# A planned kernel (attention and two MLPs): later landings in the planner's DMA model, and new tables of priorities and engine choices

## The chip, the cores and the metric

The kernel runs on one core of one Trainium2 chip. The metric is device time in microseconds (us), the median of several runs. Before the change it is 858.77 us (three runs, 855.53 to 861.29).

## The reference, cut to what matters

All data are fp32. There are 4 batches, 8 heads, 576 positions, head width 64 and 32 memory slots.

```
a    = softmax(phi over the 576 positions)              # per batch, head and memory slot
k_m  = a^T k ;  v_m = a^T v                             # 32 x 64 each
attn = softmax(q k_m^T / 8 over the 32 slots) v_m       # 576 x 64 per head
x    = attn as [2304 tokens, 512]
x    = (h * sigmoid(1.702 h)) @ w_out,  h = x @ w_in    # 512 -> 2048 -> 512
xn   = x / rms(x) * rms_g
out  = (silu(xn @ w_gate) * (xn @ w_val)) @ w_o2        # 512 -> 1536 -> 512
```

## The kernel before, in words

The tokens are worked in two pairs of batches (pair 0 and pair 1, 1152 tokens each). The time line has these stages:

- **Attention and first MLP of pair 0** (up to about 240 us). For each batch and half of the heads (a unit, such as (0,1) or (3,0)) the steps `att_k1` to `att_q4` make memory keys and values and then `attnT`. For each of eight groups of 256 hidden columns, `vm_part` folds the memory values into `w_in`, `a_g1` makes the hidden activations, `a_g2` adds into `x2`. Each fp32 operand is split into a high and a low part (the high part a rounded copy on ACT, the low part a subtraction on DVE or POOL), and each product is three matmuls, high by high, low by high and high by low.
- **First MLP of pair 1** (about 240 to 420 us), with the weights read back from `cache_a`. Beside it run pair 0's norm and `t_a`, `t_b`, `t_c`, `t_d`, which form sums and differences of quarters of `x2` and split them into the tiles `tba`, `tbb`, `tbc`, `tbd`.
- **Second MLP of pair 0** (about 420 to 640 us), then of pair 1 (to the end): `s_g3` makes the gated hidden activations of 128 columns by a scheme with seven block products, and `s_g4` multiplies them by `w_o2` and adds into `oacc`; after the last group, `put` writes the output.
- **Weights.** `w_load` (line 731) starts a DMA into one of three `raw` buffers (a strict pool: taken in a fixed order), and `w_conv` (line 766) cleans up the bits: an absolute value on ACT, two TENSOR_SCALARs and two SCALAR_TENSOR_TENSORs, then the split. The second MLP's weights are cleaned during the first MLP (`c`), kept in `cache_b`, combined in `b` and kept in `cache_s`.

**What sets the order.** All steps are first recorded as operations. A planner (class `Plan`) then makes an order for all engines together, and the instructions are issued in that order, engine by engine, each engine in order; what an instruction needs is ensured by semaphores. `cost` (line 361) gives each operation a duration by a formula. `dues` (line 452) gives each a due time: a PE step of the main line is due when its PE turn comes, a side step 20 us (`LAG`) after; then a pass backward makes each operation due early enough for everything that follows from it, or waits for its buffer. `HASTE` takes a number of us off the due time of a step's operations (negative: due later) ahead of that pass. `order` (line 493) walks along the time and, on each engine, takes of the operations that can start the one that is due first. `OTHER` lists, for a step, which of its operations (by number) go to the other one of DVE and POOL.

For a DMA the model is: the transfer starts 1.3 us after its issue, moves at 350 GB/s (224 for 96-partition tiles) one after another, and tells of its landing 0.6 us after the last byte; at most eight are under way.

```
bus = max(bus, t + 1.3) + n / (224e3 if x.ap[0][1] == 96 else 350e3)
u.done = bus + 0.6
```

For a load of 512 KB on an idle bus that is 3.4 us. `fill` (line 576) adds matmuls of `ones_r`, whose result nobody reads, wherever the plan has PE idle before a step that takes a fresh PSUM tile; so these show in the trace where the plan expected PE to stand.

Of the kernel before, what the change touches and what calls it, by code (L numbers as in the profile page):

```python
# [116 lines left out]
class Plan:  # L117
# [5 lines left out]
    SEM = 0.06  # L123
    LAG = 20.0
    FILL = True
    UNIT = {"cache_a": 131072, "cache_b": 65536, "cache_s": 131072}

    HASTE = {
        "a_g1 0 0 1": 8.9,
        "a_g1 0 1 1": 11.5,  # L130
        "a_g1 0 3 0": 26.7,
        "a_g1 0 4 0": 21.9,
        "a_g1 0 4 2": 15.4,
        "a_g1 0 5 0": 20.6,
        "a_g2 0 0 3": 10.5,
        "a_g2 0 1 0": 9.5,
        "a_g2 0 1 1": 13.3,
        "a_g2 0 2 2": 24.1,
        "a_g2 1 5 1": 110.4,
        "att_k1t 1 1": 68.1,  # L140
        "att_k2 2 1": 41.5,
        "att_k3 0 0": 99.0,
        "att_k5 0 1": 38.0,
        "att_k5 2 1": -47.3,
        "att_q3 1 0 0": 45.5,
        "att_q3 1 0 1": 79.0,
        "att_q3s 2 1 0": 3.1,
        "att_q3s 2 1 1": 35.7,
        "att_q3s 3 0 0": 35.3,
        "att_q3s 3 0 1": 54.3,  # L150
        "att_q4 1 0 0": 30.7,
        "att_q4 1 1 0": 43.8,
        "att_q4 2 0 0": 17.4,
        "att_q4 2 1 0": -93.1,
        "norm_1 1 0": 48.0,
        "norm_4 0 0 3": 80.3,
        "norm_4 0 2 3": 123.5,
        "rg": -72.1,
        "s_g3 0 0 1": 19.6,
        "s_g3 1 4 1": 131.2,  # L160
        "s_g4 0 0 1": 26.1,
        "s_g4 0 0 6": 52.3,
        "s_g4 1 1 5": 145.9,
        "s_g4 1 5 7": -42.9,
        "t_b 0 0": 25.2,
        "t_c 0 0": 4.1,
        "vm_part 0 5 0": 29.8,
        "w_conv a 0 0 in 1": 62.1,
        "w_conv a 0 3 out 1": 37.3,
        "w_conv a 0 4 in 0": 32.2,  # L170
        "w_conv b 10 o2": 118.9,
        "w_load a 0 1 out 1": 44.7,
        "w_load a 0 5 in 1": 60.7,
        "w_load b 1 vg": 116.0,
        "w_load c 2 val 1": 115.6,
        "w_load c 3 val 0": 100.1,
    }

    OTHER = {
        "a_g1 0 0 0": (17,),  # L180
        "a_g1 0 0 1": (17,),
        "a_g1 0 1 0": (8,),
        "a_g1 0 1 1": (8,),
        "a_g1 0 1 3": (17,),
        "a_g1 0 2 0": (8, 17),
        "a_g1 0 2 1": (8, 10, 21),
        "a_g1 0 2 2": (8, 10, 19),
        "a_g1 0 3 0": (8,),
        "a_g1 0 3 1": (10,),
        "a_g1 0 3 2": (8, 10, 21),  # L190
        "a_g1 0 3 3": (8, 17),
        "a_g1 0 4 0": (17,),
        "a_g1 0 4 1": (10, 19),
        "a_g1 0 5 0": (17,),
        "a_g1 0 5 1": (10, 19),
        "a_g1 0 5 2": (8, 19, 21),
        "a_g1 0 6 0": (8,),
        "a_g1 0 6 1": (10,),
        "a_g1 0 6 2": (8, 19, 21),
        "a_g1 0 7 1": (8,),  # L200
        "a_g1 1 1 0": (8,),
        "a_g1 1 1 3": (8, 17),
        "a_g1 1 2 1": (21,),
        "a_g1 1 2 3": (17,),
        "a_g1 1 4 1": (21,),
        "a_g1 1 4 2": (8,),
        "a_g1 1 4 3": (17,),
        "a_g1 1 5 0": (8,),
        "a_g1 1 5 1": (19, 21),
        "a_g1 1 5 2": (19, 21),  # L210
        "a_g1 1 6 0": (17,),
        "a_g1 1 6 1": (8, 21),
        "a_g1 1 6 2": (19,),
        "att_k3 1 0": (2,),
        "att_k3 1 1": (2,),
        "att_k3 2 0": (2,),
        "att_k3 2 1": (2,),
        "att_k3s 1 0": (1, 2),
        "att_k3s 1 1": (2,),
        "att_k4 1 0": (27,),  # L220
        "att_k4 1 1": (27,),
        "att_k4 3 0": (27,),
        "att_k4 3 1": (27,),
        "att_q3s 0 0 0": (1,),
        "att_q3s 0 1 0": (1,),
        "att_q3s 0 1 1": (1,),
        "att_q3s 1 0 1": (1,),
        "att_q3s 1 1 1": (1,),
        "att_q3s 2 0 0": (3,),
        "att_q3s 2 0 1": (3,),  # L230
        "att_q3s 2 1 0": (3,),
        "att_q3s 2 1 1": (1, 3),
        "att_q3s 3 0 0": (1, 3),
        "norm_1 0 0": (2,),
        "norm_1 0 1": (5,),
        "norm_1 0 2": (2, 5),
        "norm_1 1 0": (5,),
        "norm_1 1 1": (2, 5),
        "norm_1 1 2": (3, 5),
        "s_g3 0 0 2": (33, 35, 38, 43),  # L240
        "s_g3 0 1 2": (28, 30, 35, 36, 41),
        "s_g3 0 11 2": (31, 33, 35),
        "s_g3 0 2 2": (33, 35, 38, 40, 43),
        "s_g3 0 3 2": (30, 31, 36, 40),
        "s_g3 0 5 2": (40,),
        "t_a 0 0": (1, 3),
        "t_b 0 0": (1,),
        "t_b 0 1": (1,),
        "t_c 0 0": (5,),
        "t_c 0 1": (1, 4, 5, 7),  # L250
        "t_c 1 0": (1, 4),
        "t_c 1 1": (5,),
        "w_conv a 0 0 in 0": (1,),
        "w_conv a 0 0 out 0": (1,),
        "w_conv a 0 0 out 1": (6,),
        "w_conv a 0 1 in 0": (1,),
        "w_conv a 0 1 out 0": (1,),
        "w_conv a 0 1 out 1": (1,),
        "w_conv a 0 2 in 0": (6,),
        "w_conv a 0 2 in 1": (1, 6),  # L260
        "w_conv a 0 2 out 0": (6,),
        "w_conv a 0 3 in 0": (6,),
        "w_conv a 0 3 in 1": (6,),
        "w_conv a 0 3 out 1": (1,),
        "w_conv a 0 4 out 0": (1, 6),
        "w_conv a 0 4 out 1": (1,),
        "w_conv a 0 5 in 1": (1,),
        "w_conv a 0 5 out 0": (1,),
        "w_conv a 0 5 out 1": (1,),
        "w_conv a 0 6 in 1": (1,),  # L270
        "w_conv a 0 6 out 0": (1,),
        "w_conv a 0 6 out 1": (1, 6),
        "w_conv a 0 7 in 1": (6,),
        "w_conv a 0 7 out 0": (1,),
        "w_conv a 0 7 out 1": (1, 6),
# [4 lines left out]
        "w_conv b 3 vg": (2, 3, 11),  # L280
        "w_conv b 4 vg": (2, 5),
        "w_conv b 5 vg": (5,),
        "w_conv b 8 vg": (5,),
        "w_conv c 0 o2 0": (1,),
        "w_conv c 0 val 0": (1,),
        "w_conv c 1 o2 0": (1,),
        "w_conv c 1 o2 1": (1,),
        "w_conv c 1 val 1": (1,),
        "w_conv c 2 gate 0": (1,),
        "w_conv c 2 gate 1": (1,),  # L290
        "w_conv c 2 val 0": (1,),
        "w_conv c 3 gate 0": (1,),
        "w_conv c 3 gate 1": (1,),
        "w_conv c 3 val 0": (1,),
        "w_conv c 3 val 1": (1,),
# [26 lines left out]
    def add(self, op):  # L322
# [6 lines left out]
        for x, write in [(x, False) for x in op.ins] + [(op.out, True)]:  # L329
# [163 lines left out]
    def order(self, until=1e9):  # L493
# [9 lines left out]
        while got < len(units):  # L503
            best = None
            for e in self.ENGINES:
# [20 lines left out]
            t, u = best  # L526
# [18 lines left out]
            if e == "SP":  # L545
                x = u.ops[0].out if u.ops[0].out.space != bass.MemoryType.DRAM else u.ops[0].ins[0]
                n = reduce(int.__mul__, (c for s, c in x.ap), 4)
                bus = max(bus, t + 1.3) + n / (224e3 if x.ap[0][1] == 96 else 350e3)
                u.done = bus + 0.6
                lanes = lanes[1:] + [u.done]  # L550
            for h in u.takes:
                tag = h.tag
# [1234 lines left out]
```

## Time and profile before

| | |
|---|---|
| median of 3 runs | 858.77 us (855.53, 858.77, 861.29) |
| profiled execution | 859.84 us, span 858.1 us, mean granted TensorE clock 0.989 |
| PE busy | 835.6 us (97% of the span), 5785 matmuls |
| DVE busy | 646.2 us (75%) |
| ACT busy | 498.6 us (58%) |
| POOL busy | 288.6 us (34%) |
| DMA | 167.00 MB, mean 195 GB/s |

The span is the time from the first to the last instruction; the execution's own time is 1.7 us longer. An engine is busy while it works on an instruction. For PE, 97% is a union of overlapping matmuls and also counts the matmuls on `ones_r`. The clock is 1.0 at 2.4 GHz and 0.5 at 1.2 GHz.

### The profile page before, as it was taken

To read this page: it belongs to the slowest core of one execution; us is meant where nothing else is said; L and a number is where in the kernel's file an instruction comes from. 1 tells how busy PE (TensorE), PEld (TensorE's weight loads), DVE (VectorE), ACT (ScalarE), POOL (GpSimd) and SP (SyncE) were. 2 spreads that over 40 slices of the span, in tenths; PEclk is the share of its full clock that TensorE was granted. 3 is DMA by queue.
4 is the path that set the end of the run, shared out by engine and by line. 5 is a ranking of instruction groups with operands and counts; after the bars stand their busy time and mean duration, and the time that the engine had idled before them with its cause. 6 is when DMAs were issued, how large, how long until landed. Compare 5 with 4: busy or idle time off the path is not lost.

```text
span 858.1 us, 16008 instructions
## 1 busy us (share of the span) xinstructions
PE 835.6 (97%) x5785; PEld 791.8 (92%) x5785; DVE 646.2 (75%) x1367; ACT 498.6 (58%) x1223; POOL 288.6 (34%) x291
## 2 busy tenths in 40 slices
PE   9999999989999999999899999999999999999997
PEld 7899999989899999999899899999999999999996
DVE  6789999889896898899877698686877434555455
ACT  4698767867688667656577765444444443423321
POOL 4364346786455575746645520000020000000000
PEclk9899999999999999999999999999999999999999
DMA  9965747864975865664775658453544624434403
GB/s 337 270 218 146 251 168 203 265 210 148 303 235 175 263 210 200 238 207 145 253 250 171 234 182 326 150 215 137 216 149 143 216 95 155 170 129 130 159 1 111
DMA packets 76768, 167.00 MB, mean 195 GB/s; under 512 B 7312, under 2 KB 29328, under 8 KB 76688
## 3 DMA queue, kind: packets, MB, share of 16 engines
q1 hardware_dynamic: 76688, 165.97, 58.5%
q8 instruction: 46, 0.75, 0.4%
q14 instruction: 34, 0.28, 0.1%
HBM read 106.69 MB, written 59.24 MB: 193 GB/s over the span
## 4 chain that ended last, share of the span: by engine, by line
PE 75%; DVE 7%; DMA 7%; ACT 4%; issue 3%; POOL 2%; SPq 1%; ACTq 0%; DVEq 0%; POOLq 0%
PE pg L608 39%; PE ps_A L608 20%; PE ps_S L608 8%; PE pq L608 3%; PE pk L608 3%; PE pvm L608 2%; DMA raw_a_out<-in_moe_w_out_dram 2%; DMA stage<-in_q_dram 1%; DVE pad L608 1%; DVE x L608 1%; DVE cv L608 1%; DMA raw_b_vg<-cache_b 1%; POOL a_inl L608 1%; DVE stage L608 1%; ACT L608 1%
## 5 line engine op out<-in xcount | busy, mean ns | idle before, releaser
L608 PE MATMUL pg<-gr,a_outh 128*128 128x384 f32 (+1 forms) x736 | 197.8, 337 | 1.0 <-POOL gr L608 0.9
L608 PEld LDWEIGHTS pg<-gr,a_outh 128*128 128x128 f32 x736 | 134.1, 189 | 2.3 <-POOL gr L608 1.4
L608 POOL TENSOR_TENSOR gr<-gf,gr 128x96 fp32r<-128x96 f32 (+2 forms) x132 | 101.4, 785 | 98.9 <-ACT gr L608 75.0
L608 PE MATMUL pg<-gr,a_outl 128*128 128x384 f32 (+1 forms) x368 | 122.7, 333 | 0.0
L608 ACT COPY c<-ps_A 128x256 f32<-128x256 f32 (+1 forms) x144 | 57.0, 399 | 104.9 <-PE ps_A L608 100.7
L608 PE MATMUL pg<-s_o,pp 128*128 128x512 f32 x432 | 114.2, 392 | 0.0
L608 DVE TENSOR_TENSOR x<-x,pg 128x384 f32<-128x384 f32 (+1 forms) x172 | 88.8, 538 | 15.8 <-PE pg L608 14.4
L608 DVE TENSOR_TENSOR oacc<-oacc,pg 128x512 f32<-128x512 f32 x90 | 61.5, 686 | 44.9 <-PE pg L608 43.7
L608 PEld LDWEIGHTS pg<-s_o,pp 128*128 128x128 f32 x432 | 78.8, 188 | 14.8 <-POOL pp L608 0.2
L608 PE MATMUL ps_A<-tba,s_A 128*128 128x256 f32 (+1 forms) x576 | 86.6, 297 | 0.7 <-ACT s_A L608 0.3
L608 PEld LDWEIGHTS ps_A<-tba,s_A 128*128 128x128 f32 x576 | 80.5, 190 | 2.7 <-ACT s_A L608 0.8
L608 DVE TENSOR_TENSOR c<-c,ps_S 128x320 f32<-128x320 f32 (+1 forms) x96 | 42.8, 451 | 48.6 <-ACT c L608 33.6
L608 ACT ACTIVATE gf<-pg 128x288 f32<-128x288 f32 x128 | 51.0, 412 | 38.3 <-PE pg L608 27.3
L608 PEld LDWEIGHTS pg<-gr,a_outl 128*128 128x128 f32 x368 | 69.8, 190 | 0.0
L608 ACT CAST gr<-gf 128x288 fp32r<-128x288 f32 (+2 forms) x184 | 59.6, 362 | 12.2 <-PE pg L608 9.8
L608 PE MATMUL pg<-s_o,tbd 128*128 128x512 f32 x216 | 61.2, 392 | 0.0
L608 DVE TENSOR_TENSOR c<-c 128x320 f32<-128x320 f32 (+1 forms) x90 | 42.0, 478 | 16.8 <-ACT c L608 15.2
L608 PE MATMUL ps_A<-tbb,s_S 128*128 128x320 f32 (+1 forms) x288 | 45.6, 298 | 3.2 <-POOL tbb L608 1.7
L608 PEld LDWEIGHTS ps_A<-tbb,s_S 128*128 128x128 f32 x288 | 41.7, 190 | 5.5 <-POOL tbb L608 1.9
L608 PE MATMUL ps_A<-tbc,s_S 128*128 128x320 f32 (+1 forms) x288 | 45.6, 300 | 0.4 <-DMA s_S<-cache_s 0.4
L608 PE MATMUL ps_A<-tbd,s_A 128*128 128x320 f32 (+1 forms) x288 | 44.7, 296 | 1.0 <-ACT c L608 1.0
L608 PEld LDWEIGHTS pg<-s_o,tbd 128*128 128x128 f32 x216 | 39.1, 188 | 6.8
(231 smaller groups left out, 1856.9 us busy)
## 6 DMA issues: line engine op xcount, KB each, us to landing
cache_s<-s_S SPq DMA_DIRECT2D x24, 512.0 KB, 4.1
s_S<-cache_s SPq DMA_DIRECT2D x24, 512.0 KB, 3.7
cache_b<-cv SPq DMA_DIRECT2D x36, 256.0 KB, 4.8
raw_a_in<-in_moe_w_in_dram SPq DMA_DIRECT2D x16, 512.0 KB, 6.0
raw_a_out<-in_moe_w_out_dram SPq DMA_DIRECT2D x16, 512.0 KB, 4.5
raw_c_gate<-in_moe_w_gate_dram SPq DMA_DIRECT2D x12, 512.0 KB, 4.6
raw_c_val<-in_moe_w_val_dram SPq DMA_DIRECT2D x12, 512.0 KB, 5.1
raw_c_o<-in_moe_w_out_dram SPq DMA_DIRECT2D x12, 512.0 KB, 4.5
```

Source lines behind the costliest of these rows:

```text
L608: getattr(self.real[op.eng], op.name)(*op.args, **op.kw)
```

## The change

The constant 0.6 us in the DMA model becomes `DLAT`, 1.4 us. The two tables are new. `HASTE` goes from 48 entries to 59. `OTHER` goes from 179 operations that change engine to 223: 105 are kept, 74 dropped and 118 new. Of the 223, 120 go from DVE to POOL (before 96), and 103 from POOL to DVE (before 83). By kind:

| operations in the other engine's queue | before | after |
|---|---|---|
| low parts of `a_g1`, 288 columns, POOL to DVE | 20 | 30 |
| low parts of `a_g1`, 192 or 96 columns, POOL to DVE | 32 | 36 |
| first TENSOR_SCALAR of `w_conv a` and `c`, DVE to POOL | 34 | 40 |
| 576-column operations of `t_a` to `t_d`, DVE to POOL | 12 | 17 |
| sums and low parts of `w_conv b`, DVE to POOL | 17 | 23 |
| `s_g3`, DVE to POOL | 22 | 27 |

No operation is added to or taken from the computation; tiles, pools and cost formulas are the same. The fillers on `ones_r` are set anew by the plan.

```diff
+    DLAT = 1.4
 ...
     HASTE = {
-        "a_g1 0 0 1": 8.9,
+        "a_g1 0 0 1": 19.4,
 ...
-        "att_k5 0 1": 38.0,
+        "att_k5 0 1": 60.2,
 ...
+        "ld_src 0 0 1": 71.5,
 ...
-        "rg": -72.1,
+        "rg": -33.5,
 ...
-        "s_g4 1 5 7": -42.9,
+        "s_g3 1 11 1": 57.9,
+        "s_g3 1 11 2": -61.0,
+        "s_g4 1 5 0": -73.1,
 ...
-        "t_b 0 0": 25.2,
-        "t_c 0 0": 4.1,
+        "t_a 0 1": 70.9,
+        "t_b 0 1": 59.7,
+        "t_c 0 0": 31.9,
+        "t_d 0 1": 42.8,
 ...
-        "w_load a 0 1 out 1": 44.7,
-        "w_load a 0 5 in 1": 60.7,
-        "w_load b 1 vg": 116.0,
+        "w_load a 0 0 in 1": 81.8,
+        "w_load a 0 1 out 1": 56.9,
+        "w_load a 0 4 out 1": 55.7,
+        "w_load a 0 5 in 1": 66.5,
+        "w_load b 1 vg": 141.7,
 ...
     OTHER = {
-        "a_g1 0 2 0": (8, 17),
+        "a_g1 0 2 0": (17,),
 ...
-        "t_c 0 0": (5,),
         "t_c 0 1": (1, 4, 5, 7),
 ...
-                u.done = bus + 0.6
+                u.done = bus + self.DLAT
```

## Rows read from the trace of the kernel before

**Rows 1.** Busy time by stage: length, PE, PEld, DVE, ACT, POOL, clock, DMA share, GB/s.

```profile
0.00:60.00 60.00, 57.24 (x547) 50.86 (x547) 45.76 (x120) 39.97 (x99) 29.79 (x39) 0.91 0.90 277
60.00:240.00 180.00, 171.70 (x1361) 165.80 (x1360) 161.21 (x344) 135.51 (x325) 100.88 (x92) 1.00 0.66 211
240.00:420.00 180.00, 178.52 (x1181) 177.28 (x1180) 155.14 (x296) 121.43 (x300) 105.71 (x112) 1.00 0.65 217
420.00:500.00 80.00, 75.22 (x475) 69.65 (x474) 62.44 (x121) 56.05 (x121) 41.99 (x41) 0.96 0.61 208
500.00:858.10 358.10, 352.87 (x2231) 328.25 (x2229) 221.68 (x491) 145.61 (x380) 10.28 (x10) 1.00 0.46 159
```

**Rows 2.** Time line at the end: ACT, PE, DVE.

```profile
838.98 0.44 ACT L608 ACTIVATE c<-ps_A 128x320 f32<-128x320 f32 x1 [3.76 <-PE ps_A L608]
...
841.04 12.43 PE L608 MATMUL pg<-s_o,pp 128*128 128x512 f32 x54
...
844.63 0.42 DVE L608 TENSOR_TENSOR pp<-c,pp 128x256 fp32r<-128x256 f32 x1
```

**Rows 3.** Fillers on `ones_r`: duration min/median/max ns, first and last start, forms.

```profile
L608 PE MATMUL pvm<-ones_r x16: 222/381/775, 30.8 to 38.6; 128*128 128x512 f32 x14, 128*128 128x128 f32 x2
```

**Rows 4.** The waits of PE, 60 to 240 us: total, times, longest.

```profile
PE pvm L608 <- POOL a_inl L608: 2.8, 2, 1.7
PE pk L608 <- DMA stage<-in_q_dram: 1.9, 1, 1.9
```

**Rows 5.** The windows around the change of stage at 420 us, columns as in Rows 1.

```profile
422.00:427.20 5.20, 2.06 (x10) 1.50 (x9) 5.20 (x11) 2.24 (x4) 4.13 (x3) 0.85 0.68 199
427.20:433.00 5.80, 5.80 (x23) 5.80 (x23) 3.75 (x7) 2.17 (x6) 4.17 (x4) 0.55 0.61 221
```

**Rows 6.** Time line, 411 to 427 us: start, us, engine, operation [idle before <-releaser].

```profile
411.22 0.33 SPq L608 DMA_DIRECT2D raw_c_o<-in_moe_w_out_dram  x1
...
417.12 0.67 ACT L608 ACTIVATE cv<-raw_c_o 128x512 f32<-128x512 f32 x1 [3.77 <-DMA raw_c_o<-in_moe_w_out_dram]
...
417.82 0.43 DVE L608 TENSOR_SCALAR cv<-cv 128x512 f32<-128x512 f32 x1 [2.75 <-ACT cv L608]
...
422.74 0.75 DVE L608 TENSOR_TENSOR x<-x 128x576 f32<-128x576 f32 x1
...
425.33 1.40 POOL L608 TENSOR_TENSOR tbb<-x,tbb 128x576 fp32r<-128x576 f32 x1
```

**Rows 7.** The page's DMA issues: count, KB each, median us from issue to landing.

```profile
s_S<-cache_s SPq DMA_DIRECT2D x24, 512.0 KB, 3.7
...
raw_a_in<-in_moe_w_in_dram SPq DMA_DIRECT2D x16, 512.0 KB, 6.0
```

**Rows 8.** Groups by form, DVE and POOL: busy us, mean ns, idle before.

```profile
L608 DVE SCALAR_TENSOR_TENSOR pad<-raw_a_out,pad 128x512 uint32<-128x512 uint32 x32 | 25.8, 805 | 0.2
...
L608 DVE TENSOR_SCALAR pad<-pad 128x512 f32<-128x512 f32 x15 | 8.3, 559 | 2.0 <-ACT pad L608 2.0
...
L608 DVE TENSOR_TENSOR gr<-gf,gr 128x288 fp32r<-128x288 f32 x20 | 11.1, 562 | 0.2 <-ACT gr L608 0.2
L608 DVE TENSOR_TENSOR x<-x 128x576 f32<-128x576 f32 x11 | 10.5, 960 | 0.0
...
L608 POOL TENSOR_TENSOR gr<-gf,gr 128x288 fp32r<-128x288 f32 x52 | 53.2, 1032 | 51.3 <-ACT gr L608 34.9 <-PE pg L608 5.6 <-issue 4.7
L608 POOL TENSOR_SCALAR pad<-pad 128x512 f32<-128x512 f32 x17 | 37.4, 2198 | 13.9 <-ACT pad L608 12.1 <-PE pg L608 1.7
...
L608 POOL TENSOR_TENSOR x<-x 128x576 f32<-128x576 f32 x5 | 7.6, 1510 | 2.7 <-DVE x L608 2.7
```

**Rows 9.** Time line at the start: ACT, then DVE.

```profile
8.11 0.66 ACT L608 ACTIVATE pad<-raw_a_in 128x512 f32<-128x512 f32 x1 [1.34 <-DMA raw_a_in<-in_moe_w_in_dram]
...
14.40 0.77 DVE L608 TENSOR_TENSOR y<-kmisc 128x192 f32<-128x192 f32 x1 [2.08 <-DMA kmisc<-in_phi_dram]
```

**Rows 10.** Time line of DVE at 347 us, POOL being busy from 344.72 to 348.82.

```profile
347.00 1.36 DVE L608 TENSOR_TENSOR x<-x 128x576 f32<-128x576 f32 x1
```

More of the change, by code (lines that the diff above doesn't have):

```diff
@@ L125 @@
     FILL = True
+    DLAT = 1.4
     UNIT = {"cache_a": 131072, "cache_b": 65536, "cache_s": 131072}
     HASTE = {
-        "a_g1 0 0 1": 8.9,
+        "a_g1 0 0 1": 19.4,
         "a_g1 0 1 1": 11.5,
-        "a_g1 0 3 0": 26.7,
+        "a_g1 0 1 2": 21.4,
+        "a_g1 0 3 0": 26.4,
         "a_g1 0 4 0": 21.9,
-        "a_g1 0 4 2": 15.4,
-        "a_g1 0 5 0": 20.6,
-        "a_g2 0 0 3": 10.5,
+        "a_g1 0 5 0": 26.3,
+        "a_g2 0 0 2": 16.5,
+        "a_g2 0 0 3": 13.2,
         "a_g2 0 1 0": 9.5,
-        "a_g2 0 1 1": 13.3,
@@ L138 @@
-        "a_g2 0 2 2": 24.1,
+        "a_g2 0 2 0": 23.0,
+        "a_g2 0 2 2": 27.6,
         "a_g2 1 5 1": 110.4,
-        "att_k1t 1 1": 68.1,
-        "att_k2 2 1": 41.5,
-        "att_k3 0 0": 99.0,
-        "att_k5 0 1": 38.0,
[L144 to L157, printed above, removed]
-        "rg": -72.1,
-        "s_g3 0 0 1": 19.6,
-        "s_g3 1 4 1": 131.2,
-        "s_g4 0 0 1": 26.1,
-        "s_g4 0 0 6": 52.3,
-        "s_g4 1 1 5": 145.9,
-        "s_g4 1 5 7": -42.9,
-        "t_b 0 0": 25.2,
-        "t_c 0 0": 4.1,
-        "vm_part 0 5 0": 29.8,
-        "w_conv a 0 0 in 1": 62.1,
-        "w_conv a 0 3 out 1": 37.3,
@@ L170 @@
-        "w_conv a 0 4 in 0": 32.2,
-        "w_conv b 10 o2": 118.9,
-        "w_load a 0 1 out 1": 44.7,
-        "w_load a 0 5 in 1": 60.7,
-        "w_load b 1 vg": 116.0,
+        "att_k1 2 1": 45.4,
+        "att_k2 2 1": 35.4,
+        "att_k3 0 0": 96.8,
+        "att_k5 0 1": 60.2,
+        "att_k5 2 0": 7.8,
+        "att_q1 2 1 0": 0.3,
+        "att_q3 1 0 0": 43.2,
+        "att_q3 1 0 1": 81.5,
+        "att_q3s 2 1 0": 3.9,
+        "att_q3s 2 1 1": 35.9,
+        "att_q3s 3 0 0": 35.4,
@@ new lines @@
+        "att_q3s 3 0 1": 59.0,
+        "att_q4 1 1 0": 43.7,
+        "att_q4 2 0 0": 22.2,
+        "att_q4 2 1 1": 4.4,
+        "att_q4 3 1 1": 69.4,
+        "ld_src 0 0 1": 71.5,
+        "norm_1 1 0": 52.8,
+        "norm_4 0 0 3": 83.8,
+        "norm_4 0 2 3": 123.2,
+        "rg": -33.5,
+        "s_g3 0 0 1": 28.9,
+        "s_g3 0 7 2": 67.1,
+        "s_g3 1 0 2": 116.4,
+        "s_g3 1 11 1": 57.9,
+        "s_g3 1 11 2": -61.0,
+        "s_g4 0 0 5": 45.2,
+        "s_g4 0 0 6": 52.3,
@@ new lines @@
+        "s_g4 0 1 4": 58.8,
+        "s_g4 0 5 5": 80.4,
+        "s_g4 1 4 2": 131.2,
+        "s_g4 1 5 0": -73.1,
[3 more added lines that the diff above has]
+        "t_d 0 1": 42.8,
+        "vm_part 0 5 0": 29.8,
+        "w_conv a 0 0 in 1": 62.2,
+        "w_conv c 5 gate 1": 36.4,
+        "w_conv c 5 o2 0": 48.2,
+        "w_load a 0 0 in 1": 81.8,
+        "w_load a 0 1 out 1": 56.9,
+        "w_load a 0 4 out 1": 55.7,
+        "w_load a 0 5 in 1": 66.5,
@@ L175 @@
+        "w_load b 1 vg": 141.7,
         "w_load c 2 val 1": 115.6,
-        "w_load c 3 val 0": 100.1,
+        "w_load c 3 val 0": 126.6,
     }
@@ L180 @@
         "a_g1 0 0 0": (17,),
-        "a_g1 0 0 1": (17,),
[2 rows of a table added]
         "a_g1 0 1 0": (8,),
         "a_g1 0 1 1": (8,),
-        "a_g1 0 1 3": (17,),
-        "a_g1 0 2 0": (8, 17),
-        "a_g1 0 2 1": (8, 10, 21),
[4 rows of a table added]
         "a_g1 0 2 2": (8, 10, 19),
@@ L190 @@
         "a_g1 0 3 2": (8, 10, 21),
-        "a_g1 0 3 3": (8, 17),
[1 row of a table added]
         "a_g1 0 4 0": (17,),
[L193 to L206, printed above, removed]
-        "a_g1 1 4 3": (17,),
[L208 to L213, printed above, removed]
[31 rows of a table added]
         "att_k3 1 0": (2,),
@@ L217 @@
         "att_k3 2 1": (2,),
-        "att_k3s 1 0": (1, 2),
-        "att_k3s 1 1": (2,),
[3 rows of a table added]
         "att_k4 1 0": (27,),
-        "att_k4 1 1": (27,),
-        "att_k4 3 0": (27,),
         "att_k4 3 1": (27,),
         "att_q3s 0 0 0": (1,),
[1 row of a table added]
         "att_q3s 0 1 0": (1,),
         "att_q3s 0 1 1": (1,),
[L227 to L236, printed above, removed]
-        "norm_1 1 0": (5,),
[L238 to L245, printed above, removed]
[23 rows of a table added]
         "t_a 0 0": (1, 3),
[1 row of a table added]
         "t_b 0 0": (1,),
         "t_b 0 1": (1,),
-        "t_c 0 0": (5,),
[2 rows of a table added]
         "t_c 0 1": (1, 4, 5, 7),
-        "t_c 1 0": (1, 4),
-        "t_c 1 1": (5,),
[3 rows of a table added]
         "w_conv a 0 0 in 0": (1,),
-        "w_conv a 0 0 out 0": (1,),
[1 row of a table added]
         "w_conv a 0 0 out 1": (6,),
         "w_conv a 0 1 in 0": (1,),
[L257 to L263, printed above, removed]
[7 rows of a table added]
         "w_conv a 0 3 out 1": (1,),
@@ L267 @@
         "w_conv a 0 5 in 1": (1,),
-        "w_conv a 0 5 out 0": (1,),
-        "w_conv a 0 5 out 1": (1,),
-        "w_conv a 0 6 in 1": (1,),
[3 rows of a table added]
         "w_conv a 0 6 out 0": (1,),
-        "w_conv a 0 6 out 1": (1, 6),
-        "w_conv a 0 7 in 1": (6,),
[3 rows of a table added]
         "w_conv a 0 7 out 0": (1,),
-        "w_conv a 0 7 out 1": (1, 6),
-        "w_conv b 0 vg": (5, 14),
[3 rows of a table added]
         "w_conv b 1 vg": (0, 1, 11),
-        "w_conv b 2 vg": (2, 8, 11, 14),
[2 rows of a table added]
         "w_conv b 3 o2": (1,),
[L280 to L283, printed above, removed]
[3 rows of a table added]
         "w_conv c 0 o2 0": (1,),
         "w_conv c 0 val 0": (1,),
[2 rows of a table added]
         "w_conv c 1 o2 0": (1,),
         "w_conv c 1 o2 1": (1,),
-        "w_conv c 1 val 1": (1,),
         "w_conv c 2 gate 0": (1,),
         "w_conv c 2 gate 1": (1,),
-        "w_conv c 2 val 0": (1,),
         "w_conv c 3 gate 0": (1,),
```

95 rows, old and new, of the table OTHER are left out of this document.

## The prediction

> **What bounds the kernel now.** I read the busy time by stage, then the fillers and PE's waits stage by stage, and last the time line around the largest wait. PE's busy times over the five stages add up to 835.6 of 858.1 us [rows 1], and no matmul of the computation goes away, so a new order can win only PE's idle time, stretches at the low clock, and fillers. The stages differ in idle time (length less PE busy): 2.8 us up to 60 us, 8.3 from 60 to 240, 1.5 from 240 to 420, 4.8 from 420 to 500, and 5.2 after that. Of the last, 4.6 us is the tail: PE's last matmuls end at 841.04 + 12.43 = 853.5 of 858.1 [rows 2]. From 500 us on PE is therefore full, and the tables can win at most 0.6 us in 360. Everything is decided in the first 500 us, where DVE is the second engine: busy 161.2 of 180 us (90%) from 60 to 240 [rows 1].
>
> How much of this did the plan of before know? Fillers stand where it expected PE to be idle ahead of a fresh PSUM tile, and the last of them starts at 38.6 us [rows 3]. The waits of `pvm` on the low part of a weight (2.8 us, POOL) and of `pk` on `q` (1.9 us, DMA) [rows 4] are of that kind, come much later, and have no filler. The chip ran late against the plan there. So the idle time after 60 us is mostly surprise, and surprise is what tables searched under disturbance could lessen.
>
> **The change, term by term.** Positive is gain.
>
> *1. The change of stage at 420 us.* From 422 to 427.2 us PE works 2.06 us, so 3.1 us are idle; in the windows from 422 to 433 the clock reads 0.85 and 0.55 [rows 5], which makes 0.30 x 5.2 + 0.90 x 5.8 = 6.8 us at the low of the two levels, right behind idle PE. After 427.2 PE has no idle time, so 5.2 us of it cost 2.6 us more than at full clock. Together 5.7 us. The cause can be followed backward [rows 6]. PE waited for the low part of T2 (a product of `t_c 0 1`) made by POOL at 425.33; that came from a subtraction on DVE at 422.74; DVE had stood idle 2.75 us until 417.82 behind a cleaning step that waited for ACT, and ACT had waited 3.77 us for a load issued at 411.22, that is 5.9 us from issue to use. The planner's formula gave such a load 3.4 us on an idle bus, and gives 4.2 now; the medians on the chip are 3.7 us for one kind of 512 KB load and 6.0 for another [rows 7]. The new tables also make the chain start earlier: `t_d 0 1` is hastened by 42.8 us, it reads the quarter that `t_c 0 1` writes last, and the backward pass hands that on to the subtraction of 422.74; `t_b 0 1` and `t_c 0 0` are earlier too. The split of T2 itself has no haste, but with its input there it needs only an idle moment of ACT and POOL. Bounds 0 and 5.7; I take 5.0, nearer the upper end, because both the late load and the late subtraction are met.
>
> *2. From 60 to 240 us.* 8.3 us idle in about a dozen waits, the largest listed [rows 4]. The wait for `q` is a late load by itself, and the formula's 3.4 us against 6.0 for `raw_a_in` [rows 7] can have made others through the cleaning of the weights. But DVE's own formula is left as it was: it gives a SCALAR_TENSOR_TENSOR of 512 columns 0.075 + 512/960 = 0.61 us, and the row says 0.81 [rows 8]. With DVE at 90% this lateness stays. Bounds 0 and 8.3; I take half, 4.1.
>
> *3. The other idle time*: 1.5 from 240 to 420, 4.8 - 3.1 = 1.7 from 420 to 500, 0.6 later, together 3.8 us; again half, 1.9.
>
> *4. The start.* Loads run one behind another. `att_k5 0 1` is hastened by 60.2 us instead of 38.0, which pulls the `phi` and `k` of unit (0,1) forward, and DVE waited 2.08 us for that `phi` [rows 9]: a gain of up to 2.1. On the other side `ld_src 0 0 1` (`v`) and half of `w_in` are hastened by 71.5 and 81.8; if they pass the first `phi`, it lands two loads later, and two 512 KB loads in a row reached ACT 0.66 + 1.34 = 2.0 us apart (ACT's work on the first, then its wait for the second) [rows 9], so the loss is up to 4.0. I take +1.5, because `phi` (0,0) is held in front by `att_k3 0 0` (96.8 us) through the backward pass.
>
> *5. DVE and POOL.* Ten more low parts of 288 columns on DVE cost it 10 x 0.56 = +5.6 us and relieve POOL of 10.3; five more operations of 576 columns and six more first TENSOR_SCALARs on POOL cost it 5 x 1.51 + 6 x 2.2 = 20.8 and relieve DVE of 5 x 0.96 + 6 x 0.56 = 8.2 [rows 8]. Net about -3 for DVE and +10 for POOL, which has idle time to cover it; if that cover fails it adds 1.5 or 2.2 us to a chain, one operation. An operation of DVE on `x` took 1.36 us next to a busy POOL [rows 10], its mean is 0.96 [rows 8], and one took 0.75 [rows 6]; so a meeting costs DVE 0.2 us as a mean and 0.6 at worst. With some 15 more meetings that is 3 us of DVE, of which I put 1.0 on PE's path (bounds 0 and 3).
> The Trainium skill (SBUF — State Buffer, section "Who interferes with whom") says that a DVE instruction with two SBUF inputs and a GpSimd instruction that reads SBUF exclude each other for the whole instruction. By that rule POOL's added 10 us could hold DVE for as long, 7 us more than I count, and the median below would be 856.5; the rows show meetings of 0.2 us as a mean, and I go by them.
>
> *6. New waits.* A plan at 97% of PE puts steps just in time, and DVE's lateness of term 2 will find other ones. Nearest row: 8.3 us over about a dozen waits makes some 0.7 us each [rows 1]; I take three, -2.2 (bounds 0 and -8.3, the same again).
>
> *7. The end.* `s_g3 1 11 2` is put later and the block 0 of the last `s_g4` is put last. From ACT at 838.98 to DVE's last low part at 844.63 + 0.42 the chain takes 6.1 us [rows 2], now under the last products and blocks. If two blocks of 12.43/9 = 1.4 us are all that covers it, 3.3 us come out; I take 0, since other `s_g4` blocks are left to stand there.
>
> **Sum.** 5.0 + 4.1 + 1.9 + 1.5 - 1.0 - 2.2 = 9.3 us. Against the profiled execution: 859.84 - 9.3 = 850.5. That execution is 1.1 us over the median of the runs shown, so the median comes to 858.8 - 9.3 = 849.5 us. All upper ends give 5.7 + 8.3 + 3.8 + 2.1 = 19.9 us, 838.9; about 1% (8.6 us: 850.2 and 867.4) is what can be told from no change.
>
> **Rivals.**
> *A, given back:* the change of stage is mended (+5.0), but from 60 to 240 us as many waits come as go, since the plan's DVE is as optimistic as before; with -1 for term 5 this is about 855. For it: DVE at 90%, formula unchanged. Against it: the late loads are met everywhere.
> *B, nothing reaches PE:* half of the 223 engine choices are new, each of the old waits has a new one in its place, or PE's waits were set by other operations of the same steps (T2's split has no entry of its own). Then 858.8, give or take 3.
> *C, slower: weights run ahead of the attention.* Four `w_load a` steps are hastened by 56 to 82 us, and the strict pool of three raw buffers hands that on to every load and cleaning before them. Each half costs DVE two TENSOR_SCALARs and two SCALAR_TENSOR_TENSORs, 2 x 0.56 + 2 x 0.81 = 2.7 us [rows 8]. Four halves ahead of a softmax step of units (2,0) to (3,1), between 120 and 240 us, are 10.9 us; DVE has 18.8 us idle in the whole stage [rows 1] and can't take that at one place. With 2 us of other matmuls as cover PE stands 8.9 us, and two stretches at the low clock of 2.6 each, as behind the idle time at 422 [rows 5], make 14.1; with term 1 still won the loss is 9.1, some 868. It decides from about three halves on. Against it: the same kind of entries stood in the table before, and gave waits of 1.7 and 1.9 us at most [rows 4].
>
> **How the numbers follow.** Forecast (about 843 to 850): 0.47. A: 0.24. B: 0.14. C: 0.15. Faster by over 1% is the forecast's case without its upper edge and nothing of A: 0.46. Slower by over 1% is C: 0.14. Within 1% is the rest: 0.40. The range from 842 to 864 leaves out C (0.14) and about 0.05 below, where nearly all idle time would go; it takes in the bounds of terms 4 and 7 around A and B.
>
> **What would show it.** Term 1: no idle PE and a clock of 1.0 around 420 to 433, and the subtraction of T2 long before its use. Term 2: less than 5 us idle from 60 to 240, POOL's low parts of weights and the late `q` gone from the waits. Term 4: `phi` of (0,1) reaching DVE before 13 us, and fillers ending earlier. Term 5: DVE's 576-column mean near 0.96. Term 7: the last 54 matmuls still without a gap. The prediction is wrong if PE's idle time after 60 us stays at 15 us or more, or if a second stretch at the low clock appears after 60 us.

## The result, and the profile after

The changed kernel takes 846.28 us (median of 4 runs, 843.96 to 847.96), the one before 858.05 (4 runs, one more than in the table ahead of the prediction, 855.53 to 861.29): the ratio is 0.9859, 95% interval 0.9817 to 0.9901, 11.8 us less. The profiled executions lie further apart, 859.84 and 843.96 us: 15.9 us, since that of before is 1.8 above its median and that of after is its fastest run. The two traces below therefore have 4 us more to explain than the medians.

PE's busy time by stage of the changed kernel, in the columns of [rows 1]:

```profile
0.00:60.00 60.00, 53.30 (x541) 47.97 (x542) 48.91 (x124) 39.22 (x98) 27.29 (x36) 0.94 0.90 277
60.00:240.00 180.00, 177.84 (x1421) 172.18 (x1421) 169.87 (x351) 138.53 (x338) 96.14 (x91) 1.00 0.69 223
240.00:420.00 180.00, 179.21 (x1174) 178.13 (x1173) 163.63 (x315) 121.24 (x296) 104.68 (x105) 1.00 0.66 217
420.00:500.00 80.00, 79.86 (x535) 75.48 (x534) 69.31 (x132) 58.73 (x132) 40.18 (x38) 1.00 0.64 219
500.00:842.20 342.20, 337.33 (x2127) 313.61 (x2126) 203.37 (x444) 136.25 (x360) 28.12 (x26) 1.00 0.46 157
```

Length less PE busy gives 6.7, 2.2, 0.8, 0.1 and 4.9 us idle, 14.7 in all; before it was 2.8, 8.3, 1.5, 4.8 and 5.2, which is 22.6. So 7.9 of the 15.9 us are idle time, and the rest is busy time: PE is busy 827.5 us instead of 835.6 with the same products. Of that, fillers give 2.5 us (12.0 instead of 14.5). The low clock gives at most 5: the stretches at the lower level add up to 6.8 us here and to 17 before, and half of the 10 us between them is what full speed would have saved, had PE never waited in them.

Three windows of the changed kernel, same columns: the only stretch at the low level (41.8 to 48.6 us), and the two that answer to [rows 5]:

```profile
41.90:48.70 6.80, 6.14 (x32) 6.02 (x33) 4.02 (x10) 4.56 (x15) 2.14 (x3) 0.51 1.01 319
422.00:427.20 5.20, 5.20 (x38) 5.14 (x36) 4.76 (x10) 2.71 (x6) 3.31 (x2) 1.00 0.79 216
427.20:433.00 5.80, 5.80 (x45) 5.63 (x44) 4.67 (x9) 5.04 (x10) 1.29 (x1) 1.00 0.82 290
```

At 422 to 433 us PE works all the time at a clock of 1.00, where it had worked 7.86 of 11.0 us at 0.85 and 0.55. The low stretch now lies in the start.

All the waits of PE that are over 0.3 us in total (total, times, longest):

```profile
PE pk L644 <- DVE kmisc L644: 2.0, 6, 0.5
PE pk L644 <- DMA stage<-in_k_dram: 1.8, 1, 1.8
PE pk L644 <- ACT kz L644: 1.3, 2, 1.0
PE pk L644 <- DVE ones_r L1604: 1.3, 1, 1.3
PE pq L644 <- ACT stage L644: 0.9, 1, 0.9
PE pvm L644 <- DVE a_inl L644: 0.8, 1, 0.8
PE pg L644 <- POOL gr L644: 0.8, 2, 0.6
```

The waits of [rows 4] are gone: POOL's low part and the late `q` are not in the list, and nothing after 60 us is longer than 0.8 us. What is new stands in the start (`in_k`, `kz`).

The fillers, as in [rows 3], and the end, as in [rows 2]:

```profile
L644 PE MATMUL pk<-ones_r x27: 217/382/793, 1.3 to 164.2; 128*128 128x512 f32 x20, 128*128 128x128 f32 x7
...
L644 PE MATMUL pvm<-ones_r x16: 220/381/462, 28.2 to 35.3; 128*128 128x512 f32 x14, 128*128 128x128 f32 x2
```

```profile
824.91 12.43 PE L644 MATMUL pg<-s_o,pp 128*128 128x512 f32 x54
...
828.50 0.42 DVE L644 TENSOR_TENSOR pp<-c,pp 128x256 fp32r<-128x256 f32 x1
```

By the time line the last filler of the start stands at 36.3 instead of 38.6 us; three of the 27 in the first row stand at 163.7 to 164.2 us (0.7 us of PE), the only ones that the new plan has after 60 us. The last 54 matmuls run without a gap, 12.43 us as before, and DVE's last low part is done 8.4 us ahead of their end in both kernels.

### The profile page after: what moved, and what is told of

The parts are those of the page before. It is cut to its first block, busy times and chain, and to the rows that moved or that the text cites. A ratio compares the mean times of both kernels' runs of the same rounds, so it can differ in the third digit from the quotient of the medians.

```text
span 842.2 us, 16000 instructions
## 1 busy us (share of the span) xinstructions
PE 827.5 (98%) x5789; PEld 787.4 (93%) x5789; DVE 655.1 (78%) x1363; ACT 494.0 (59%) x1222; POOL 296.4 (35%) x295
## 4 chain that ended last, share of the span: by engine, by line
PE 78%; DVE 10%; DMA 4%; issue 3%; ACT 3%; POOL 2%; SPq 0%; POOLq 0%; ACTq 0%; DVEq 0%
PE pg L644 42%; PE ps_A L644 21%; PE ps_S L644 9%; DVE pad L644 3%; PE pvm L644 2%; DVE x L644 2%; PE pq L644 2%; PE pk L644 1%; DMA stage<-in_q_dram 1%; DVE kmisc L644 1%; DVE stage L644 1%; DVE cv L644 1%; DMA stage<-in_v_dram 1%; DMA raw_c_gate<-in_moe_w_gate_dram 1%; DMA raw_a_out<-in_moe_w_out_dram 1%
## 5 line engine op out<-in xcount | busy, mean ns | idle before, releaser
L644 PE MATMUL pg<-gr,a_outh 128*128 128x384 f32 (+1 forms) x736 | 195.2, 334 | 0.8 <-POOL gr L644 0.6
L644 POOL TENSOR_TENSOR gr<-gf,gr 128x288 fp32r<-128x288 f32 (+2 forms) x118 | 83.8, 727 | 101.1 <-ACT gr L644 52.4
L644 ACT COPY c<-ps_A 128x320 f32<-128x320 f32 (+1 forms) x144 | 57.2, 399 | 93.7 <-PE ps_A L644 91.8
L644 PE MATMUL ps_A<-tba,s_A 128*128 128x320 f32 (+1 forms) x576 | 88.5, 296 | 0.0
L644 DVE TENSOR_TENSOR c<-c 128x256 f32<-128x256 f32 (+1 forms) x86 | 39.3, 466 | 18.3 <-ACT c L644 16.6
L644 POOL TENSOR_SCALAR pad<-pad 128x512 f32<-128x512 f32 x20 | 41.2, 2062 | 19.9 <-ACT pad L644 19.7
L644 POOL TENSOR_SCALAR cv<-cv 128x512 f32<-128x512 f32 x20 | 44.1, 2210 | 8.1 <-ACT cv L644 6.5
L644 PE MATMUL ps_A<-tbc,s_S 128*128 128x256 f32 (+1 forms) x288 | 46.0, 297 | 0.0
L644 PE MATMUL ps_S<-tbb,s_S 128*128 128x256 f32 (+1 forms) x288 | 45.8, 296 | 0.0
```

The costliest lines, as they stand in the source:

```text
L644: getattr(self.real[op.eng], op.name)(*op.args, **op.kw)
```

## The experiments

The prediction's own reason was lateness: the plan of before expected transfers too early, so its waits were surprises. Three theories came out of it. **Landings:** the constant (1.4 instead of 0.6 us) mends the plan by itself. **Backlog:** DVE, or one late chain on it (T2's subtraction), is what PE waits for. **Fit:** the two tables are fitted to one plan, constant included, and only the three together have a value. A fourth question is how much the new order stands when transfers land late. Times are medians; a ratio is against the kernel before, run beside it on the same chip, with its 95% interval.

**1. Old tables with the new constant.** In the kernel before:

```
-                u.done = bus + 0.6
+                u.done = bus + 1.4
```

> The old tables, the DMA constant alone changed from 0.6 to 1.4 us. Theory L (the plan before took landings too early, and that alone made PE wait): idle PE after 60 us falls from 15 us to about 8, the stretch at the low clock at 425 us is gone, 849 to 852 us. Theory T (the gain is in the new tables, searched for steps that bear lateness; old tables in another plan fit nothing): 855 to 865 us, idle PE after 60 us at 12 us or more, in other places than before.

Measured: 856.13 us, 0.9993 [0.9957, 1.0028]. The constant alone gives nothing, but it takes nothing from the old tables either. The wait at 422 us does go, but another comes. The time line of PE in this kernel (start, busy us, operation, idle before and its releaser):

```profile
450.59 1.97 PE L609 MATMUL ps_A<-tbd,s_A 128*128 128x320 f32 x6 [3.24 <-ACT c L609]
...
453.96 3.14 PE L609 MATMUL pg<-ones_r 128*128 128x512 f32 x9
```

A wait of 3.24 us at 450.59, and right behind it nine fillers: this plan expects idle time there, and part of it is still a surprise. It has 59 fillers of 17.3 us against 41 of 14.5.

**2. New tables with the old constant.** In the changed kernel:

```
-    DLAT = 1.4
+    DLAT = 0.6
```

> The new tables, the DMA constant back at 0.6 us. Theory L: the landings surprise the plan again, waits behind loads come back, 853 to 858 us. Theory T: the tables were searched with landings disturbed, so 0.8 us less in the plan does little: 845 to 850 us, no low clock after 60 us.

Measured: 879.74 us, 1.0251 [1.0194, 1.0307]. Its largest wait is 5.17 us at 442.18 (`ps_S` on DVE's `x`), and of its 73 fillers 29 stand after 60 us, between 141 and 467.

**3 and 4. One table new, one old, constant 1.4.**

```
     HASTE = { ... }     # 3: of the changed kernel; 4: of the kernel before
     OTHER = { ... }     # 3: of the kernel before;  4: of the changed kernel
```

> Constant 1.4 us, the new priorities, the old choices of DVE or POOL. If the gain at 420 us comes from the priorities (t_d 0 1, t_b 0 1, t_c 0 0), PE has under 1.5 us idle from 420 to 433 and no low clock there; the stages before are between the two kernels: 849 to 853 us. If the choices of engine carry it, the idle time at 420 us stays near 3 us: 855 us or more.

> Constant 1.4 us, the old priorities, the new choices of engine. If the priorities carry the gain at 420 us, the T2 subtraction is late again and PE loses 3 us or more there: 852 to 858 us. If the choices of engine carry it: 848 to 851 us.

Measured: 867.83 us, 1.0101 [1.004, 1.0162], and 881.06 us, 1.0265 [1.0192, 1.0338]. Either half of the tables alone makes the kernel slower; the longest waits are 4.78 us at 474.44 and 5.64 us at 483.84, both for `s_S` on ACT.

**5. T2 made early.** The order of before, with the operations 2 to 5 of `t_c 0 1` moved up to stand right behind `t_b 0 1`:

```
+            to = 1 + max(key.index(x) for x in (("t_b 0 1", 1), ("t_b 0 1", 2), ("t_c 0 1", 1)))
+            order = order[:to] + [order[k] for k in moved] + [...]
```

> The order of before word for word, but the four operations of t_c 0 1 that make T2 (the subtraction on DVE, the rounded copy on ACT, the subtraction and the low part on POOL) stand right behind t_b 0 1, some 30 us earlier in their queues. If the late T2 alone cost what term 1 of the prediction says: no idle PE and no low clock from 422 to 433 us, 5 to 6 us less, 850 to 853 us. If the next operation made just in time stalls there instead (DVE is as late as before): 855 to 857 us, with a new wait of 2 us or more before 450 us.

Measured: 865.65 us, 1.0082 [1.0058, 1.0106]. The loss at the change of stage stays. PE and then ACT in this kernel:

```profile
393.50 0.55 PE L616 MATMUL pg<-gr,a_outh 128*128 128x384 f32 x1 [2.37 <-ACT gr L616]
...
434.89 1.97 PE L616 MATMUL ps_A<-tbc,s_S 128*128 128x320 f32 x6 [3.45 <-ACT c L616]
```

```profile
431.27 0.68 ACT L616 ACTIVATE cv<-raw_c_gate 128x512 f32<-128x512 f32 x1 [2.94 <-DMA raw_c_gate<-in_moe_w_gate_dram]
433.90 0.62 ACT L616 CAST s_A<-raw_b_vg 128x512 fp32r<-128x512 f32 x1 [1.95 <-DMA raw_b_vg<-cache_b]
434.42 0.42 ACT L616 COPY c<-ps_A 128x320 f32<-128x320 f32 x1
```

Where the operations were put in, PE now waits 2.37 us for ACT's `gr` (393.50). And at the change of stage it waits for the next product that comes just in time: ACT's copy of `c` at 434.42 stands behind a cast that waited 1.95 us for `raw_b_vg`, behind a step that waited 2.94 us for `raw_c_gate`. So making this one chain early is not enough: in the order around it, other products come as late. The kernel is 7.5 us slower than the one before, and the wait for `gr` is one that the kernel before does not have.

**6. Fillers in the new start.** Four fillers each ahead of `att_q4 0 1 0` and `att_k5 1 0` in the changed kernel, the places of the waits at 39.95 and 42.56 us:

```
+                more = {"att_q4 0 1 0": 4, "att_k5 1 0": 4}.get(step, 0) if x[2].eng == "PE" else 0
+                ...
+                order += [(x[0], -1, Fill((held.ap[:, :512],), kw)) for i in range(more)]
```

> The order of after, with four filler matmuls on ones_r ahead of att_q4 0 1 0 and four ahead of att_k5 1 0, where PE stood 0.9 and 1.0 us idle without one at 39 to 43 us. If that idle time is what brought the low clock from 42 to 49 us: clock 1.0 there, about 3 us less, 842 to 844 us. If the clock falls whatever is done, or the fillers hold PE when its data is there: 846 to 848 us.

Measured: 846.08 us, 0.9854 [0.9808, 0.99], the same as without them (846.28). In its trace both waits are gone, and the clock is 1.0 from 33 to 60 us: the low stretch that stood at these waits is gone too. But this execution has low stretches of 3.4 and 6.8 us that begin at 15.7 and 25.9 us, ahead of the fillers, which therefore can't have made them. The start differs that much between executions of one order: 8 and 10 below have the order of the changed kernel on PE, and what their edits change begins after 60 us. The first 60 us of 8, then of 10, in the columns of [rows 1]:

```profile
0.00:60.00 60.00, 55.59 (x543) 48.57 (x544) 50.07 (x124) 39.40 (x99) 27.24 (x36) 0.97 0.89 277
```

```profile
0.00:60.00 60.00, 54.22 (x494) 48.66 (x498) 43.30 (x113) 34.15 (x82) 24.35 (x33) 0.83 0.88 275
```

The clock is 0.97 and 0.83 where the profiled execution of the changed kernel has 0.94, and the matmul that begins at 60.0 us there begins at 59.6 and at 65.2 us. Beside that, one trace can't show a gain of 3 us, and the four runs show none.

**7 and 8. Later landings.** In each order, a copy of 256 KB from memory to memory is issued ahead of each load of original weights into a `raw` buffer that is planned after 60 us, 57 in all:

```
+                if op.eng == "SP" and t > 60 and op.out.tensor.name.startswith("raw") and ...:
+                    self.real["SP"].dma_start(out=self.spare[next(late)], in_=self.other[0:128, 0:512])
```

> The order of before; ahead of each of the 57 loads of original weights after the start a DMA of 256 KB from DRAM to DRAM that nobody reads, so that landings are later by its 0.7 us or more. If the new tables bear lateness better, before loses at least twice what after loses under the same: before 863 to 870 us.

> The order of after under the same extra DMAs. If it was searched to bear late landings: a loss of 1 to 4 us, 847 to 851 us. If it only fits the chip as it is: a loss like that of before under the same, 8 us or more, 854 us or more.

Measured: the order of before takes 868.83 us, 1.0105 [1.0052, 1.0158], 10.7 more than without the copies; the new order 852.65 us, 0.9932 [0.9903, 0.9961], 6.4 more than in the result above. The loads do land later: `raw_c_gate` takes 5.8 us from issue to landing (median) instead of 4.6, in the new order 6.0 instead of 4.7. PE's largest waits, first of the order of before, then of the new one:

```profile
PE pk L611 <- DMA stage<-in_v_dram: 4.6, 1, 4.6
PE pnr L611 <- DVE r L611: 2.8, 1, 2.8
```

```profile
PE pk L647 <- DVE kmisc L647: 2.0, 3, 1.4
PE pg L647 <- POOL gr L647: 2.0, 4, 0.8
```

The old order gets a wait of 4.6 us for one load and one of 2.8 for DVE; the new one gets none over 1.4 us. It loses less, but the two losses have uncertainties of some 4 us each, so that it stands better is likely and not shown.

**9 and 10. Less work on DVE.** In either order the second SCALAR_TENSOR_TENSOR of each `w_conv c` cleans only 64 of its 512 columns, which leaves out a part of the cleaned weights. DVE is busy 15.7 us less by it in the first kernel and 19.6 in the second, not quite the 22 us of the expectation:

```
+                if key and key[0].startswith("w_conv c") and key[1] == 4:
+                    op.kw = {k: x[:, :64] if hasattr(x, "tensor") else x for k, x in op.kw.items()}
```

> The order of before; the second SCALAR_TENSOR_TENSOR of each cleaning of a second-MLP weight works on 64 of its 512 columns (the low bits of the other columns stay out of those weights), so some 36 x 0.6 = 22 us of DVE go, most of it ahead of 480 us. If a backlog on DVE is what PE waits for at the change of stage: 849 to 853 us, idle PE from 420 to 460 us under 1.5 us. If the late landings hold ACT and DVE whatever DVE has to do: 856 to 859 us, with the wait at 422 us still there.

> The order of after with the same columns left out. PE stands only 3 us between 60 and 500 us there, so less work on DVE can give little: 843 to 846 us. If more than 4 us come, DVE still bounds the new order.

Measured: 857.26 us, 0.9992 [0.9969, 1.0014], and 846.97 us, 0.9871 [0.9849, 0.9893]: no gain in either. PE in the first of them, at the place of [rows 6]:

```profile
418.02 0.89 PE L611 MATMUL ps_A<-tbb,s_S 128*128 128x320 f32 x5
421.91 0.64 PE L611 MATMUL ps_A<-tbb,s_S 128*128 128x320 f32 x1 [3.00 <-POOL tbb L611]
```

The wait for POOL's low part of T2 is still there, 3.00 us, though DVE is busy 144.7 instead of 155.1 us from 240 to 420. How much DVE has to do is not the bound at this place.

**11. The constant 0.1 us further.** In the changed kernel `DLAT = 1.5`:

> The new tables with the DMA constant 1.5 instead of 1.4 us, nearer to the landings of the trace. If the tables bear small differences of the plan: 845 to 850 us. If they fit one plan alone: 855 to 880 us, with fillers after 60 us, where the plan itself has PE stand.

Measured: 875.97 us, 1.0212 [1.0195, 1.023]: 0.1 us in one constant of the plan costs 30 us. Its fillers after 60 us, and two stages:

```profile
L644 PE MATMUL pg<-ones_r x30: 220/380/382, 170.3 to 395.0; 128*128 128x512 f32 x26, 128*128 128x128 f32 x4
...
L644 PE MATMUL ps_A<-ones_r x26: 221/381/382, 438.1 to 462.0; 128*128 128x512 f32 x23, 128*128 128x128 f32 x3
```

```profile
60.00:240.00 180.00, 174.88 (x1392) 168.99 (x1391) 162.44 (x339) 134.41 (x329) 99.24 (x89) 1.00 0.65 205
...
420.00:500.00 80.00, 71.95 (x434) 66.55 (x433) 60.40 (x112) 49.35 (x104) 40.85 (x37) 0.94 0.65 225
```

It has 106 fillers, 26.4 us, half of them between 170 and 462 us, where this kernel's plan knows that PE has nothing to do; and from 420 to 500 us PE is idle for another 8 us.

**12. No tables.** Both empty, constant 1.4:

```
+    HASTE = {}
+    OTHER = {}
```

> Both tables empty, constant 1.4 us: what the planner gives by itself. If tables that do not fit are as bad as none, near the 880 us of the mixed kernels; if they are worse than none, below 870 us; if even unfitting tables help, above 890 us.

Measured: 878.6 us, 1.0242 [1.0194, 1.0289]. Fillers:

```profile
L442 PE MATMUL pg<-ones_r x56: 220/381/463, 49.3 to 251.4; 128*128 128x512 f32 x48, 128*128 128x128 f32 x8
...
L442 PE MATMUL ps_A<-ones_r x46: 220/381/463, 448.6 to 496.3; 128*128 128x512 f32 x41, 128*128 128x128 f32 x5
```

So tables that don't fit their plan (876 to 881 us in 2, 4 and 11) are worth no more than none, and the 102 fillers of these two rows show that the bare plan expects its idle time.

**What follows.** The constant alone gives nothing (1); the new tables without it, or a half of them with it, cost 11 to 25 us (2 to 4), and 0.1 us more in the constant costs 30 (11). The landings and the backlog theory fall as they stood (1; 5 and 9). For the new tables the fit holds: in none of the four neighbouring plans (2, 3, 4 and 11) is the kernel faster than before. For the old tables it does not hold as it was stated: with a constant 0.8 us off theirs they give 856.13 us, where the planner without tables gives 878.6 (1 and 12), so they keep some 22 us of worth in a plan that is not theirs. One such pair can be luck, since the order is another one there, with other waits and 18 more fillers. The likely reason for the rest, argued and not shown, is that a planner that puts each step where its cost model finds room answers a small change with another order in many places, and that the tables are corrections to one such order. How far that goes was underestimated: 2, 4 and 5 came out 9 to 23 us above every time that was expected of them.

What stays open is why the new fit is better than the old one: that the tables were searched under disturbance, as the prediction has it, or only that a better order was found for this plan. 7 and 8 lean to the first without showing it; only searches with and without disturbance would tell.

## Why the prediction was right, by its own steps

The forecast was 849.5 us with a gain of 9.3; it came to 846.28 and 11.8. The mechanism, PE's surprise waits in the first 500 us going away, is what the trace shows. Its terms:

| Term | Predicted | Measured in the two profiled executions |
|---|---|---|
| 1 change of stage | +5.0 | +5.7: idle 3.1 to 0, clock to 1.00 |
| 2 60 to 240 us | +4.1 | +6.1: idle 8.3 to 2.2 |
| 3 other idle time | +1.9 | +2.9: 0.7 from 240 to 420, 1.6 to 500, 0.6 later |
| 4 start | +1.5 | about -1.5, see below |
| 5 DVE and POOL | -1.0 | nothing reached PE |
| 6 new waits | -2.2 | none over 0.8 us; three planned fillers, -0.7 |
| 7 end | 0 | -0.2 (tail 4.63 to 4.86) |

The last column adds up to 12.3 of 15.9 us. What the rest is stays open: the matmuls of both kernels, matched by name and turn, show the changed one gaining some 8 us between 65 and 300 us, where idle time and fillers make about 6.

The sum came nearer to the result than its terms, and that is in part luck: terms 2, 3, 5 and 6 were put too low by 1.0 to 2.0 us each, and term 4 too high by 3.0. And that these tables fit this constant, on which by 2, 3, 4 and 11 everything rests, was trusted and not derived.

**Term 1** was right in size, and its reason only in part. The prediction asked for T2's subtraction long before its use, and that is not what happened. ACT, DVE, POOL and PE around T2 in the changed kernel (start, busy, operation, idle before and its releaser):

```profile
412.68 0.74 DVE L644 TENSOR_TENSOR x<-x 128x576 f32<-128x576 f32 x1
412.80 0.68 ACT L644 ACTIVATE cv<-raw_c_gate 128x512 f32<-128x512 f32 x1 [2.03 <-DMA raw_c_gate<-in_moe_w_gate_dram]
...
413.70 0.67 ACT L644 CAST tbb<-x 128x576 fp32r<-128x576 f32 x1
...
415.77 1.44 POOL L644 TENSOR_TENSOR x<-x 128x576 f32<-128x576 f32 x1
...
417.17 1.44 POOL L644 TENSOR_TENSOR tbb<-x,tbb 128x576 fp32r<-128x576 f32 x1
...
417.83 1.96 PE L644 MATMUL ps_A<-tbb,s_S 128*128 128x320 f32 x12
```

From DVE's subtraction at 412.68 to POOL's low part, done at 417.17 + 1.44 = 418.61, the chain takes 6 us (POOL's own subtraction stands in between) and ends beside PE's twelve products of `tbb` into `ps_A`, which run from 417.83 to 419.79. It is as just-in-time as before. What changed stands ahead of it: the ACT step before it, for another load (`raw_c_gate`), waited 2.03 us instead of 3.77, and DVE didn't stand idle behind it. The loads themselves are nearly as late as before. Landings:

```profile
s_S<-cache_s SPq DMA_DIRECT2D x24, 512.0 KB, 3.5
...
raw_a_in<-in_moe_w_in_dram SPq DMA_DIRECT2D x16, 512.0 KB, 5.3
```

5.3 us against 6.0 for `raw_a_in`, 3.5 against 3.7 for `s_S` [rows 7]. And ACT still waits for them from 60 to 420 us, up to 4.3 us at a time:

```profile
ACT pad L644 <- DMA raw_a_out<-in_moe_w_out_dram: 5.5, 5, 3.9
ACT cv L644 <- DMA raw_c_o<-in_moe_w_out_dram: 5.1, 2, 4.3
...
ACT cv L644 <- DMA raw_c_gate<-in_moe_w_gate_dram: 4.9, 4, 2.0
```

So the late load was rightly read as the start of this stall, but not as the thing that the change removes: in the new order what PE needs next does not stand behind it. DVE's waits for ACT's `cv` from 60 to 420 us fell from 6.9 to 0.5 us, and DVE's idle time there from 43.7 to 26.5 (360 less its busy time in [rows 1] and above).

**Term 2** was taken at half because DVE, at 90%, was thought to keep PE late. That is the step that was mis-sized: DVE is busy 169.9 of 180 us now (94%), and PE waits a quarter as long. So here a busier DVE did not make PE wait longer, and in 9 and 10 less work on DVE did not make it wait less to any gain; that DVE now works in an order nearer to PE's needs is the reading that is left, not one that a run shows by itself. Term 3 was halved by the same reasoning, term 6 charged for it.

**Term 4** had the wrong sign. Its first half came: `phi` of (0,1) reaches DVE at 12.35 instead of 14.40 [rows 9]:

```profile
12.35 1.41 DVE L644 TENSOR_TENSOR y<-kmisc 128x192 f32<-128x192 f32 x1 [0.21 <-DMA kmisc<-in_phi_dram]
```

The loss came another way than the bounds had it, which saw the first `phi` land late. `v`, hastened by 71.5 us, is loaded ahead of the first `k` now, and PE waits for that `k`. PE in the start, of the kernel before, then of the changed one:

```profile
6.51 4.67 PE L608 MATMUL pk<-ones_r 128*128 128x512 f32 x15
...
11.12 2.19 PE L608 MATMUL pk<-stage 128*64 128x128 f32 x36
```

```profile
10.36 2.19 PE L644 MATMUL pk<-stage 128*64 128x128 f32 x36 [1.83 <-DMA stage<-in_k_dram]
...
39.95 1.55 PE L644 MATMUL pq<-twin,stage 128*128 128x64 f32 x12 [0.89 <-ACT stage L644]
...
42.56 0.69 PE L644 MATMUL pk<-ident,kz 128*128 128x128 f32 x2 [0.97 <-ACT kz L644]
```

That wait costs nothing against the kernel before: fillers stood in its place there, and the products on `stage` began at 11.12 us, 0.8 later. (Kernel 1, which loads `k` ahead of `v`, waits 2.02 us there as well.) What costs are the waits of 0.89 and 0.97 us at 40 and 42.6 us, on steps of ACT (the kernel before has 0.79 at the first place and none at the second), and the low stretch that begins in the second of them. Matched by name and turn, the matmuls that begin at 30 to 40 us in the kernel before come 3.3 us earlier in the changed one (median), in part because the kernel before has a low stretch at 26.3 to 33.1 us; those of 50 to 70 us come 1.5 us later. 7 and 9 have the order of before on PE and 8 and 10 that of after, and what their edits change begins after 60 us; over all nine pairings of these traces the matmuls of 50 to 70 us come 0.4 to 8.7 us later. So the sign was wrong, and the size changes with where the low clock falls.

**Term 5.** The rows of DVE that answer to [rows 8]:

```profile
L644 DVE SCALAR_TENSOR_TENSOR pad<-raw_a_out,pad 128x512 uint32<-128x512 uint32 x32 | 25.0, 782 | 0.1
...
L644 DVE TENSOR_TENSOR gr<-gf,gr 128x288 fp32r<-128x288 f32 x30 | 14.6, 490 | 1.5 <-ACT gr L644 1.4
...
L644 DVE TENSOR_TENSOR x<-x 128x576 f32<-128x576 f32 x10 | 8.6, 872 | 0.0
```

The mean of 576 columns is 0.87 and not near 0.96, and 288 columns take 0.49 us instead of 0.56. Still DVE as a whole is busy 655.1 us instead of 646.2 with four instructions fewer, and POOL 296.4 instead of 288.6. The prediction had weighed a rule of the Trainium skill here (SBUF — State Buffer, "Who interferes with whom": a DVE instruction with two SBUF inputs contends with a reading GpSimd instruction for a port pair that is an exclusive lock). By that rule DVE could lose as much as POOL gained. What the new choice of engines does by itself comes from counting: at the means of the kernel before, group by group, it takes 0.8 us off DVE and adds 8.3 to POOL (the prediction had 3 and 10, leaving out `w_conv b` and `s_g3`), so DVE's rise is in longer means, 7.5 us of them when instructions are added up. That is nearer to the rule's 10 than to my 3; but the means moved both ways (192-column low parts rose from 0.37 to 0.45 us, 576 columns fell), and no row shows that the rule is the cause. The time that I derived from it, 856.5 us, did not come, since DVE's time does not reach PE (10).

**The rivals.** A and B (as many waits come as go) describe kernel 1, at 856.1 us, and not this one. C, weights ahead of the attention, has no trace: the waits from 60 to 240 us are 2.2 us together. What the list of rivals lacked is what 2 to 4 and 11 show: that a plan can end 20 us slower with PE's idle time planned, fillers and all. A table that fits its plan less well would have looked the same in the diff.

## What to carry to other kernels

Idle time of the bounding engine that the plan did not expect (no filler stands there) is worth more than its length suggests. Each of the eight waits of PE of 3 us or more in the traces of 1 to 12 has a stretch of 3.4 or 6.8 us at the lower clock that begins in it or within 0.5 us behind it; count both. A table of priorities may be worth nothing in the next plan: 0.1 us in one constant lost all that the new tables gave (11), while the old ones stood 0.8 us without loss (1). So time the kernel again after every change of the cost model, and expect neither. And a wait on a chain of several engines was not mended by making one link earlier (5), nor by making one engine's work less (9): look at what stands in the queue behind the late transfer.

## What was not expected of the hardware

The clock fell behind less idle time than before. The stretch of 41.8 to 48.6 us at the lower level, in which PE is busy about 6 of 6.8 us, begins in a wait of 0.97 us, 1.8 us behind one of 0.89. In 10, which has the same order on PE, it stands in the same place of the work, from 47.2 to 54.0 us, in the second of two waits of the same lengths. In the kernel before, the stretch at 425.6 us begins in the second of two waits of 1.46 and 1.68 us, and a single wait of 1.9 us at 230 to 232 brought none; nor did waits of up to 0.8 us after 60 us in the changed kernel. In the first 60 us one order gave 3.4, 6.8 and 20.5 us of low clock in three executions (8, the changed kernel, 10), so the start of one trace is no measure for a gain of some us.

DVE got 8.9 us busier without any harm to PE, while 15.7 and 19.6 us less of DVE's busy time brought PE nothing.
